# One level against two levels of Strassen's method in the second matmul of a linear-attention and feed-forward kernel

## The chip, the core and the metric

The kernel runs on one core of a Trainium2 chip. The metric is the device time of one launch in microseconds (us). All arithmetic is in 32-bit floats. TensorE (PE) multiplies; its weight loads have a row of their own in the profile (PEld). VectorE (DVE), ScalarE (ACT) and GpSimd (POOL) do the elementwise work. SyncE (SP) and ACT issue the DMAs.

## The reference, cut to what matters

```python
q, k, v: (8, 8, 576, 64)  float32     # batch, heads, sequence, head_dim
w_in: (512, 2048), w_out: (2048, 512) # float64: float32 normals times a float64 scalar

kv  = einsum('bhsd,bhse->bhde', k, v)
out = einsum('bhsd,bhde->bhse', q, kv)
out = out / sqrt(mean(out**2, -1) + 1e-6) * g_norm
x   = out, tokens by (head, dim)      # (4608, 512)
h   = x @ w_in                        # (4608, 2048)
g   = maximum(0.01 * h, h)
return (g @ w_out).astype(float32)    # (4608, 512)
```

## The kernel before, in words

**Blocks.** The 4608 tokens are cut into nine blocks of 512. For each batch entry of 576 tokens the attention writes its normalised output, transposed, into the `xT` tiles of the blocks that it touches. The feed-forward part then takes block after block. d_ff is cut into four units `c` of 512 (two halves `h` of 256 each: `w1_sb[h][c]`, `w2_sb[h][c]`).

**The first block** (`first_block`) is multiplied in the plain way: 16 slices of 128 of d_ff, each with four `h_ps` matmuls (L86) of 512 columns, a leaky ReLU on ACT (`gT`, L560) and four `o_acc` matmuls. While it runs, the weights arrive as 64-bit floats (`load_w`, 32 jobs of 0.5 MB, SP queue, L168) and `round_w` makes 32-bit floats of them: two ACT operations (L191, L193) and four DVE operations (L194, L197, L198, L200) for each job. `between(n, half)` hands out these jobs and the attention steps of batch entry 1 among the slices.

**The other eight blocks** use one level of Strassen's method (Winograd's form: seven products in place of eight) in both matmuls. `product_h` makes the seven products of a unit for h, `product_o` the seven for the output; each product is four matmuls of 256 columns. The profile shows every one of these matmuls as two MATMUL records and two LDWEIGHTS records. So a product, a "step", is eight records, a unit is 14 steps, and there are 32 units.

- The sums of weight quarters (`sides_w1`, `sides_w2`, tiles `ws`, `wt`) are made on POOL anew in every unit: eight operations of 128x512. The sums of the activations (`sides_g`, tiles `gs`) are four more. All elementwise sums go through the helper `add` (L400).
- The PSUM results go into `g11`..`g22` (ACT copies, DVE adds, ReLU on ACT) and into the output accumulators `o` (ACT copies when fresh, else DVE adds of 128x512).
- Finished accumulators go to DRAM from the ACT queue (L538).

**Order.** The main loop writes the order out: one h step, the rest of the o steps of the unit before, five h steps, one o step, the last h step, five o steps; the attention steps of the next batch entry (`a_steps`) stand between them. Matmuls (L86), `load_pair` DMAs and the rounding are pinned to program order; other instructions are ordered by the scheduler at build time, on each engine once and for all. The engines then run strictly in that order.

**Buffers.** POOL's weight sums live in `wcomb` tiles `pair0` to `pair3`, which during the first block also hold raw 64-bit weights; temporaries of the rounding live in the `gs` tiles. There are eight PSUM banks: `ha hb hc oa ob oc` and two for attention.

Of the kernel before, what the change touches and what calls it, by code (L numbers as in the profile page):

```python
# [8 lines left out]
F32 = mybir.dt.float32  # L9
# [13 lines left out]
def kernel(  # L23
# [28 lines left out]

    nc = tc.nc
# [19 lines left out]
    stage = ctx.enter_context(tc.tile_pool(name="stage", bufs=3))  # L73
# [3 lines left out]
    wcomb = ctx.enter_context(tc.tile_pool(name="wcomb", bufs=1))  # L77
    gpool = ctx.enter_context(tc.tile_pool(name="gpool", bufs=2))
    opool = ctx.enter_context(tc.tile_pool(name="opool", bufs=2))
# [5 lines left out]
    def matmul(*args, **kw):  # L85
        pin(nc.tensor.matmul(*args, **kw))  # L86

# [30 lines left out]
    def load_first():  # L118
# [4 lines left out]
        def rows(t):  # L123
# [5 lines left out]
        ks, vs = (t + [rows(wcomb.tile([P, 4 * U * P], F32, tag=f"pair{i + j}",  # L129
                                       name="early_kv")) for i in range(2)]  # L130
                  for j, t in ((0, ks), (2, vs)))
        for way, to, src, ts, p in (
# [8 lines left out]
    zeros = gpool.tile([P, NT], F32, tag="g11", name="zeros")  # L141
# [7 lines left out]
    w2_sb = [[consts.tile([P, U, DM], F32, name=f"w2_{h}_{c}") for c in range(NC)]  # L149
             for h in range(2)]  # L150

    spare_homes = itertools.cycle(("gs1", "gs2", "gs3", "gs4"))

    def spare(n, name, dtype=F32):

        return gpool.tile([P, n], dtype, tag=next(spare_homes), name=name)

    raw_homes = itertools.cycle([(stage, "raw")] * 3 + [(wcomb, f"pair{i}") for i in range(4)])
# [11 lines left out]
    def load_f64(src):  # L170
        a, n = src.shape[-2:]
        n //= 2
        pool, tag = next(raw_homes)
        raw = pool.tile([P, a * n, 2], U32, tag=tag, name="raw")
        load(raw.rearrange("p (a n) two -> p a (n two)", a=a), src)
        return raw

    def round_f64(dst, raw):
# [11 lines left out]
        add = spare(a * n, "add", U32)  # L190
# [130 lines left out]
    def attention(b):  # L321

        qT = qTs[b] = work.tile([P, NP, S], F32, tag="qT", name="qT")
        kv_ps = kv_tiles()
        for p in range(NP):
            q_in = q_ins.pop((b, p))
            nc.vector.transpose(  # L327
                qT[:, p, :].rearrange("p (t s) -> p s t", s=T),
                q_in.rearrange("p (s d) -> p s d", d=D)[:, :, :32])
            if p % 2 == 0:  # L330
                yield
                continue
            attention_kv(b, p // 2, kv_ps)
            for i in (p - 1, p):
                nxt = (b, i + 2) if i + 2 < NP else (b + 1, i + 2 - NP)
                if nxt[0] < B:
                    load_pair(*nxt)
            yield
        copy_kv(b, kv_ps)
        yield  # L340
        for i in (b, b + 1):
            yield from tail_of(b, max(i * NT, b * S), min((i + 1) * NT, (b + 1) * S))

    def first_attention():


        idle = ps_m.tile([P, NT], F32, tag="ob", name="idle_ps")
# [8 lines left out]
        rest = [ps_m.tile([P, NP // 2, 64], F32, tag=t, name="rest_ps") for t in ("oc", "oa")]  # L356
        for j in range(3):
            load_w(j)
        for p in range(NP):
            q_in = q_ins.pop((0, p))  # L360
            q_ps = ps_m.tile([P, J - 1, 64], F32, tag=("ha", "hb", "hc", "ha")[p], name="q_ps")
# [21 lines left out]
        free = iter(("ha", "hb", "hc", "oa", "ob", "oc", "ha", "hb"))  # L383
# [5 lines left out]
        for e in range(2):  # L389
            outputs(0, 0, N2, e, sums[0], ps, spare)  # L390
        outputs(0, N2, NT, 0, sums[1], ps, spare)
        divide(0, N2, sums[0], spare)
        outputs(0, N2, NT, 1, sums[1], ps, spare)
        divide(N2, NT, sums[1], spare)
# [7 lines left out]
    def sides_w1(c):  # L402

        a11, a12 = w1_sb[0][c][:, :, :2, :], w1_sb[0][c][:, :, 2:, :]
        a21, a22 = w1_sb[1][c][:, :, :2, :], w1_sb[1][c][:, :, 2:, :]
        s12, s34 = (wcomb.tile([P, 2, U, 2, P], F32, tag=f"pair{i}", name=f"ws{i}")
                    for i in range(2))
        s1, s2, s3, s4 = s12[:, 0], s12[:, 1], s34[:, 0], s34[:, 1]
        add(nc.gpsimd, s1, a21, a22)
        add(nc.gpsimd, s2, s1, a11, True)  # L410
        add(nc.gpsimd, s3, a11, a21, True)
        add(nc.gpsimd, s4, a12, s2, True)
        return {1: a11, 2: a12, 3: s4, 4: a22, 5: s1, 6: s2, 7: s3}

    def sides_w2(c):
# [3 lines left out]
        t12, t34 = (wcomb.tile([P, 2, U, N2], F32, tag=f"pair{i}", name=f"wt{i}")  # L419
                    for i in range(2, 4))  # L420
        t1, t2, t3, t4 = t12[:, 0], t12[:, 1], t34[:, 0], t34[:, 1]
# [4 lines left out]
        return {1: b11, 2: b21, 3: b22, 4: t4, 5: t1, 6: t2, 7: t3}  # L426

    def sides_x(x):

# [8 lines left out]
        add(nc.vector, t4, b21, t2, True)  # L438
        return {1: b11, 2: b21, 3: b22, 4: t4, 5: t1, 6: t2, 7: t3}

    def sides_g(g):

        g11, g12, g21, g22 = g
        s1, s2, s3, s4 = (gpool.tile([P, U, N2], F32, tag=f"gs{i}", name=f"gs{i}")
                          for i in range(1, 5))
        add(nc.gpsimd, s1, g21, g22)
        add(nc.gpsimd, s2, s1, g11, True)
        add(nc.gpsimd, s3, g11, g21, True)
        add(nc.gpsimd, s4, g12, s2, True)
        return {1: g11, 2: g12, 3: s4, 4: g22, 5: s1, 6: s2, 7: s3}  # L450

    BANK = {1: "a", 6: "a", 7: "a", 4: "a", 2: "b", 5: "c", 3: "c"}

    def strassen(which, left, right, done):


        banks = {}
        for i in (1, 5, 2, 6, 3, 7, 4):
            first = BANK[i] not in banks
            if first:  # L460
                banks[BANK[i]] = ps_m.tile([P, 2, N2], F32, tag=f"{which}{BANK[i]}",
                                           name=f"{which}_{BANK[i]}")
            bank = banks[BANK[i]]
            for part in range(2):
                for r in range(2):
                    matmul(bank[:, part, :], lhsT=left(i, part, r), rhs=right(i, part, r),
                           start=first and part == 0 and r == 0, stop=(r == 1),
                           skip_group_check=True)
            done(i, bank)
            yield  # L470

    def product_h(c, x_sides, to):

        w_sides = sides_w1(c)
        g11, g12, g21, g22 = (gpool.tile([P, U, N2], F32, tag=f"g{i}", name=f"g{i}")
                              for i in ("11", "12", "21", "22"))
# [4 lines left out]
        def done(i, bank):  # L481
# [3 lines left out]
            elif i == 5:  # L485
                nc.scalar.copy(g22, bank)
# [3 lines left out]
            elif i == 6:  # L490
                nc.scalar.copy(g21, bank)
            elif i == 3:
                add(nc.vector, g21, bank, g21)
                relu(g21)
            elif i == 7:
                add(nc.vector, g22, bank, g22)
                relu(g22)
            else:
                relu(g12, bank)
                to.append(sides_g((g11, g12, g21, g22)))  # L500

        yield from strassen("h", lambda i, part, r: w_sides[i][:, part, r, :],
                            lambda i, part, r: x_sides[i][:, r, :], done)

    def product_o(c, g_sides, os, finish):
        w_sides = sides_w2(c)
        if c == 0:
            for key in ("11", "12", "21", "22"):
                os[key] = opool.tile([P, 2, N2], F32, tag="o", name=f"o{key}", bufs=6)

        def acc(key, bank, fresh):
            if c == 0 and fresh:
                nc.scalar.copy(os[key], bank)
            else:
                add(nc.vector, os[key], bank, os[key])

        def done(i, bank):
            for key, fresh in {1: [("11", True)], 5: [("22", True)], 2: [("11", False)],
                               6: [("12", True)], 3: [("12", False)], 7: [("22", False)],
                               4: [("21", True)]}[i]:  # L520
                acc(key, bank, fresh)
                if c == NC - 1 and {"11": 2, "12": 3, "22": 7, "21": 4}[key] == i:
                    finish(key, os[key])

        yield from strassen("o", lambda i, part, r: g_sides[i][:, r, part * P:(part + 1) * P],
                            lambda i, part, r: w_sides[i][:, r, :], done)
# [7 lines left out]
    def store(i):  # L534
        def finish(key, o):
            r0 = i * NT + (int(key[0]) - 1) * N2
            c0 = (int(key[1]) - 1) * N2
            nc.scalar.dma_start(  # L538
                out[r0:r0 + N2, c0:c0 + N2].rearrange("(t p) m -> p t m", p=P), o)
        return finish  # L540

    def first_block(between):

        accs = [ps_m.tile([P, DM], F32, tag=t, name="o_acc") for t in ("ha", "hb", "oa", "ob")]
        x, last = xTs.pop(0), None
        for n in range(2 * NC * U + 1):
            now = last
            if n < 2 * NC * U:
                c, h, u = n // (2 * U), n // U % 2, n % U
                h_ps = ps_m.tile([P, NT], F32, tag=("hc", "oc")[n % 2], name="h_ps")  # L550
# [103 lines left out]
```

## Time and profile before

| | |
|---|---|
| median of 3 runs (987.89 to 992.26) | 992.06 us |
| the profiled execution's own time | 991.89 us |
| its span | 990.2 us |
| PE, PEld busy | 958.0, 763.8 us |
| DVE, ACT, POOL busy | 435.3, 268.1, 499.0 us |
| DMA read, written | 53.1, 9.4 MB |
| first block's matmuls | 26.6 to 151.2 us |

The profile is one execution. Its time lies 1.7 us above its span and 0.2 us below the median. PE's busy time is the sum of records that overlap: a record's end is modelled and reaches into the next one. The distance from one start to the next is the price of a record: 0.216 us for 256 columns.

### The profile page before, as it was taken

How to read it: one execution, taken by the hardware profiler on the slowest of the kernel's cores; microseconds unless marked ns; L12 is line 12 of the kernel's file. 1: busy time of each engine (PE TensorE's matmuls, PEld its weight loads, DVE VectorE, ACT ScalarE, POOL GpSimd, SP SyncE). 2: the span in 40 equal slices, each digit the busy share in tenths (PEclk: the TensorE clock that was granted, in tenths of full speed). 3: DMA queues.
4: the chain of work that ended last, by engine and by line, in shares of the span. 5: the costliest groups of instructions: out<-in, count | busy, mean ns of one | idle time of the engine just before them, and what ended most of it. 6: DMA issues, size and time to landing. Idle time of an engine off the chain costs nothing.

```text
span 990.2 us, 14098 instructions
## 1 busy us (share of the span) xinstructions
PE 958.0 (97%) x5702; PEld 763.8 (77%) x5702; DVE 435.3 (44%) x688; ACT 268.1 (27%) x531; POOL 499.0 (50%) x395
## 2 busy tenths in 40 slices
PE   8899987999999999999999999999999999999997
PEld 4444435878887888888887888788878888888885
DVE  3968971264234533364335433552245322422223
ACT  3645432331124211421133113311242112112210
POOL 1000214455655665566556666565556666666642
PEclk9899999999999999999999999999999999999999
DMA  9989505300260008000610043003100010001001
GB/s 251 243 214 239 164 1 138 96 1 1 56 178 1 1 2 231 2 1 1 178 56 1 1 121 113 1 1 96 45 1 1 1 43 1 1 1 43 1 1 42
DMA packets 36160, 63.47 MB, mean 64 GB/s; under 512 B 4864, under 2 KB 21248, under 8 KB 36096
## 3 DMA queue, kind: packets, MB, share of 16 engines
q1 hardware_dynamic: 26112, 51.95, 19.9%
q10 hardware_dynamic: 9856, 10.62, 3.2%
q8 instruction: 45, 0.74, 0.3%
q14 instruction: 19, 0.16, 0.1%
q0 software_dynamic: 128, 0.00, 0.0%
HBM read 53.12 MB, written 9.44 MB: 63 GB/s over the span
## 4 chain that ended last, share of the span: by engine, by line
PE 90%; DVE 6%; DMA 2%; ACT 1%; issue 1%; SPq 0%; ACTq 0%; DVEq 0%
PE h_a L86 22%; PE o_a L86 21%; PE h_c L86 11%; PE o_c L86 11%; PE h_b L86 6%; PE o_b L86 6%; PE o_acc L86 5%; PE h_ps L86 5%; PE kv_ps L86 2%; PE o_ps L86 2%; DVE qT L327 1%; DVE sum L289 1%; DMA k_in<-in_k_dram 1%; DMA v_in<-in_v_dram 1%; DMA raw<-in_moe_w_in_dram 1%
## 5 line engine op out<-in xcount | busy, mean ns | idle before, releaser
L400 DVE TENSOR_TENSOR o<-o_a,o 128x512 f32<-128x512 f32 x104 | 71.5, 688 | 122.2 <-PE o_a L86 122.2
L86 PE MATMUL o_a<-wt,gs 128*128 128x256 f32 x512 | 122.1, 381 | 0.0
L400 POOL TENSOR_TENSOR ws<-w 128x512 f32<-128x512 f32 x32 | 44.3, 1385 | 136.6 <-PE h_a L86 97.1
L400 POOL TENSOR_TENSOR wt<-w,w 128x512 f32<-128x512 f32 x32 | 40.9, 1277 | 140.5 <-PE o_a L86 137.4
L86 PEld LDWEIGHTS o_a<-wt,gs 128*128 128x128 f32 x512 | 96.3, 190 | 15.2 <-issue 2.1
L479 ACT ACTIVATE g<-g 128x512 f32<-128x512 f32 x96 | 60.5, 630 | 167.4 <-DVE g L400 167.4
L400 POOL TENSOR_TENSOR gs<-g,g 128x512 f32<-128x512 f32 x64 | 81.3, 1270 | 23.0 <-ACT g L479 22.5
L400 POOL TENSOR_TENSOR ws<-w,w 128x512 f32<-128x512 f32 x32 | 41.9, 1310 | 97.4 <-DMA raw<-in_moe_w_in_dram 94.6
L484 ACT COPY g<-h_a 128x512 f32<-128x512 f32 x32 | 18.7, 585 | 255.5 <-PE h_a L86 244.4
L400 POOL TENSOR_TENSOR wt<-w,wt 128x512 f32<-128x512 f32 x64 | 83.4, 1303 | 2.5
L400 POOL TENSOR_TENSOR wt<-w 128x512 f32<-128x512 f32 x32 | 41.2, 1289 | 65.6 <-PE o_a L86 60.0
L86 PE MATMUL h_a<-xt,w 128*128 128x256 f32 x256 | 62.6, 388 | 7.8 <-DVE g L400 7.8
L86 PE MATMUL h_ps<-xT,w 128*128 128x512 f32 (+1 forms) x136 | 60.5, 589 | 8.1 <-DVE xT L308 4.8
L400 DVE TENSOR_TENSOR g<-h_b,g 128x512 f32<-128x512 f32 x32 | 22.1, 689 | 98.0 <-PE h_b L86 98.0
L400 DVE TENSOR_TENSOR o<-o_c,o 128x512 f32<-128x512 f32 x56 | 38.4, 685 | 57.6 <-PE o_c L86 57.6
L86 PE MATMUL o_a<-wt,g 128*128 128x256 f32 x256 | 60.8, 380 | 1.9 <-DVE o L400 1.9
L86 PE MATMUL h_a<-xT,ws 128*128 128x256 f32 x256 | 62.4, 386 | 0.0
L86 PEld LDWEIGHTS h_a<-xt,w 128*128 128x128 f32 x256 | 48.8, 193 | 17.2 <-DVE g L400 10.6
L86 PE MATMUL h_a<-xT,w 128*128 128x256 f32 x256 | 62.0, 386 | 0.0
L86 PE MATMUL o_a<-w,g 128*128 128x256 f32 x256 | 60.6, 379 | 0.8 <-DVE o L400 0.8
L86 PE MATMUL h_a<-xt,ws 128*128 128x256 f32 x256 | 61.1, 382 | 0.0
L86 PE MATMUL o_c<-wt,gs 128*128 128x256 f32 x256 | 60.8, 381 | 0.0
(86 smaller groups left out, 1741.1 us busy)
## 6 DMA issues: line engine op xcount, KB each, us to landing
out_dram<-o ACTq DMA_DIRECT2D x36, 256.0 KB, 2.2
v_in<-in_v_dram SPq DMA_DIRECT2D x30, 288.0 KB, 5.0
raw<-in_moe_w_in_dram SPq DMA_DIRECT2D x64, 128.0 KB, 5.5
raw<-in_moe_w_out_dram SPq DMA_DIRECT2D x16, 512.0 KB, 6.2
k_in<-in_k_dram SPq DMA_DIRECT2D x28, 288.0 KB, 3.5
q_in<-in_q_dram SPq DMA_DIRECT2D x56, 144.0 KB, 4.5
q_in<-in_q_dram SPq DMA_DIRECT2D x56, 140.0 KB, 4.6
k_in<-in_k_dram ACTq DMA_DIRECT2D x2, 288.0 KB, 9.2
```

Of the source, the lines that this page charges most:

```text
L86: pin(nc.tensor.matmul(*args, **kw))
L289: nc.vector.tensor_add(sums[l], sums[l], sq)
L327: nc.vector.transpose(qT[:, p, :].rearrange("p (t s) -> p s t", s=T), q_in.rearrange("p (s d) -> p s d", d=D)[:, :, :32])
L400: eng.tensor_tensor(out_, a, b_, op=ALU.subtract if minus else ALU.add)
L479: nc.scalar.activation(t, t if src is None else src, func=AF.Prelu, alpha=SLOPE)
L484: nc.scalar.copy(g11, bank)
```

## The change

The first matmul keeps one level of Strassen's method. The second gets two: every product of halves becomes seven products of quarters, 49 in a unit, each one matmul of 128x128 by 128 columns. For every j of the outer seven (a "step" again) these are four matmuls into a PSUM tile `o_a` (128x512) and three into `o_b` (128x384).

- **Weights.** All sums of weights are made once: `sum_w1` (four POOL sums) and `sum_w2` (four POOL sums, three ACT copies, eight DVE sums) for each of the four units, handed out by `between` as soon as all rounding jobs have been handed out. The blocks are written to DRAM tiles (`w1_dram`, `w2_dram`: 4 and 14 DMAs for a unit, 1.05 and 3.21 MB, SP queue) and are read back for every block of tokens into rings: `w1_ring` with 6 places, `w2_ring` with 5, each read issued when the step that used the place is done.
- **Activations.** `sides_g` makes the second level's sums: eight POOL operations (four of 512, four of 384 columns) on top of the four of the first level.
- **Accumulators.** Each o step adds `o_a` and `o_b` into `acca` and `accb` (DVE, or ACT when fresh). `outputs_of` combines the seven second-level products after the last unit: 28 DVE sums of 128x128 for a block, then the store, now from the SP queue (the last block: SP and ACT).
- **Order.** h and o steps alternate, one of each; an attention step follows every second pair.
- **Places.** The pools `stage`, `wcomb`, `gpool`, `opool` are gone; fixed places serve several uses. The `tall` tile of `sum_w2` is a single place in `w2_ring`, overlapping two of the eight places for raw weights; the `w2_sb` tiles share places with `ga` and `acca`.

```diff
-    def sides_w1(c):   ...
-    def sides_w2(c):   ...
+    def sum_w1(c):
+        a11, a12, a21, a22 = w1_blocks(c)
+        s = {i: view(spare(NT, "ws"), 0, U, 2, P) for i in (1, 2, 3, 4)}
+        add(nc.gpsimd, s[1], a21, a22)
...
+    def sum_w2(c):
+        b11, b12 = w2_sb[0][c][:, :, :N2], w2_sb[0][c][:, :, N2:]
+        b21, b22 = w2_sb[1][c][:, :, :N2], w2_sb[1][c][:, :, N2:]
+        tall = {"a": view(w2_ring, 7 * P, 4, U, N2), "b": view(w2_ring, 7 * P + 4 * U * N2, 3, U, N2)}
+        t1, t2, t3, t4 = tall["a"][:, 3], tall["b"][:, 0], tall["b"][:, 2], tall["a"][:, 2]
+        add(nc.gpsimd, t1, b12, b11, True)
+        add(nc.gpsimd, t2, b22, t1, True)
+        add(nc.gpsimd, t3, b22, b12, True)
+        add(nc.gpsimd, t4, b21, t2, True)
+        nc.scalar.copy(tall["a"][:, 0], b11)
+        nc.scalar.copy(tall["a"][:, 1], b21)
+        nc.scalar.copy(tall["b"][:, 1], b22)
+        for g, n in (("a", 4), ("b", 3)):
...
+            add(nc.vector, u1, c12, c11, True)
+            add(nc.vector, u2, c22, u1, True)
+            add(nc.vector, u4, c21, u2, True)
+            add(nc.vector, c12, c22, c12, True)
+        def write():
+            for j in ORDER:
+                for g, lo, hi in (("a", 0, 4), ("b", 4, 7)):
+                    pin(nc.sync.dma_start(w2_dram[c][j][:, lo:hi, :], terms[g][j]))
...
+    def product_o(q, g_sides):
+        for t, j in enumerate(ORDER):
+            w = o_place(7 * q + t)
+            for g, lo, tags in (("a", 0, ("o0", "o1")), ("b", 4, ("o2", "o3"))):
...
+                for m in range(n):
+                    matmul(bank[:, m, :], lhsT=g_sides[g][j][:, m, :], rhs=w[:, lo + m, :],
+                           start=j in FRESH and m == 0, stop=True, skip_group_check=True)
+                to = accs[g][:, kl]
+                if c == 0 and fresh:
+                    nc.scalar.copy(to, bank)
+                else:
+                    add(nc.vector, to, bank, to)
+            read_o(7 * q + t + R2)
+            if c == NC - 1 and j in (2, 7, 3, 4):
+                outputs_of(i, kl, accs)
+            yield
+    def outputs_of(i, kl, accs):
...
+        for to, a in ((p2, p1), (p6, p1), (p7, p6), (p6, p5), (p4, p7), (p7, p5), (p3, p6)):
+            add(nc.vector, to, to, a)
...
     def between(n, half):
...
+        if rounded == len(w_jobs):
+            todo = next(sums, None)
+            if len(writes) > 1 or todo is None and writes:
+                writes.pop(0)()
+            if todo:
+                writes.append(todo[0](todo[1]))
...
     first_block(between)
+    for n in range(R1):
+        read_h(n)
+    for write in writes:
+        write()
+    for n in range(R2):
+        read_o(n)
...
+            for t in range(7):
+                go(h_steps, 1)
+                go(o_steps, 1)
+                if (7 * c + t) % 2:
+                    go(a_steps, 1)
```

## The prediction

> **What bounds the kernel now.** I read the busy times, the chain of waits, stretches of the span, prices of single groups, and last the timeline around the stage that changes.
>
> ```profile
> PE 958.0 (97%) x5702; PEld 763.8 (77%) x5702; DVE 435.3 (44%) x688; ACT 268.1 (27%) x531; POOL 499.0 (50%) x395
> PE 90%; DVE 6%; DMA 2%; ACT 1%; issue 1%; SPq 0%; ACTq 0%; DVEq 0%
> 100.00:125.00 25.00, 25.00 (x101) 10.18 (x100) 23.37 (x35) 11.58 (x24) 5.54 (x4) 1.00 0.54 147
> 125.00:151.00 26.00, 23.39 (x69) 9.82 (x68) 19.29 (x33) 7.40 (x17) 4.42 (x3) 1.00 0.03 10
> 151.00:230.00 79.00, 69.98 (x481) 57.33 (x480) 29.12 (x46) 23.36 (x48) 37.97 (x30) 0.94 0.27 71
> 430.00:534.00 104.00, 102.87 (x655) 87.05 (x654) 44.27 (x68) 26.55 (x54) 61.42 (x48) 1.00 0.21 56
> ```
>
> TensorE is 97% busy and 90% of the chain. The last four lines are stretches (length; busy us of PE, weight loads, DVE, ACT, POOL; granted clock; DMA share; GB/s). In the eight Strassen blocks PE has no air, while DVE, POOL and DMA have much. In the first block DVE is nearly full up to 125 us. Prices next: groups (count, sum in us, mean ns, idle before), one kind of DMA (us to landing), and rows of the timeline (start us, us, engine):
>
> ```profile
> L400 DVE TENSOR_TENSOR o<-o_a,o 128x512 f32<-128x512 f32 x104 | 71.5, 688 | 122.2 <-PE o_a L86 122.2
> L400 POOL TENSOR_TENSOR gs<-g,g 128x512 f32<-128x512 f32 x64 | 81.3, 1270 | 23.0 <-ACT g L479 22.5
> L400 DVE TENSOR_TENSOR xt<-xT 128x512 f32<-128x512 f32 x8 | 10.2, 1277 | 7.2 <-PE h_c L86 7.2
> L400 DVE TENSOR_TENSOR xT<-xT 128x512 f32<-128x512 f32 x8 | 5.5, 690 | 0.2
> L289 DVE TENSOR_TENSOR sum<-sum,sq 128x128 f32<-128x128 f32 x4 | 1.0, 273 | 0.0
> out_dram<-o ACTq DMA_DIRECT2D x36, 256.0 KB, 2.2
> 92.58 1.80 SPq L168 DMA_DIRECT2D raw<-in_moe_w_in_dram  x4
> 142.82 0.60 ACT L560 ACTIVATE gT<-h_ps 128x512 f32<-128x512 f32 x1 [3.91 <-PE h_ps L86]
> 141.97 1.59 POOL L400 TENSOR_TENSOR ws<-w,ws 128x512 f32<-128x512 f32 x1
> 142.47 1.64 DVE L200 CUSTOM_DVE_ANT_0 w<-w,add 128x1024 uint16<-128x1024 uint16 x1
> 145.66 0.69 DVE L200 CUSTOM_DVE_ANT_0 w<-w,add 128x1024 uint16<-128x1024 uint16 x1
> 264.69 1.28 PE L86 MATMUL kv_ps<-v_in,k_in 64*64 64x64 f32 x72
> 701.68 1.89 PE L86 MATMUL h_c<-xt,ws 128*128 128x256 f32 x8
> 703.41 0.81 PE L86 MATMUL h_b<-xT,w 128*128 128x256 f32 x3
> 706.65 1.70 PEld L86 LDWEIGHTS h_c<-xT,ws 128*128 128x128 f32 x8
> 708.95 1.59 PEld L86 LDWEIGHTS h_a<-xT,ws 128*128 128x128 f32 x8
> ```
>
> A DVE operation with two SBUF operands takes 0.69 us alone and 1.2 to 1.6 us while POOL works (the two L200 rows, one beside a POOL sum; the two `xT` groups); one that reads PSUM stays at 0.69. An SP issue costs 0.45 us. A step of eight records lasts 703.41 - 701.68 = 1.73 us, 0.216 us each. The two weight-load rows differ by 0.11 us: after a pause the second load starts 0.108 us after the first, so a 128-column load occupies 0.108 us and is hidden under 0.216 us of streaming.
>
> **The change part by part.**
>
> *The o step.* 28 matmuls of 256 columns become 49 of 128 for a unit: 14 records in a step in place of eight, half as long. Streaming is 0.216 / 2 = 0.108 us, and so is the load: the cover that hid loads is gone, both must run at once without a seam. The nearest row is `kv_ps`: 64-column loads before 64-column matmuls on four quarters of the array, 18 records on each in about 1.06 us (1.28 less the 0.22 us of a record's tail), 0.059 us each where streaming alone is 0.216 x 64/256 = 0.054. So a record costs 0.108 at best, 0.118 by that ratio; I take 0.110, as the excess looks like a fixed few ns. A step: 14 x 0.110 = 1.54 us against 1.73; 224 steps save 42 us (17 to 48). PE is on the path, so this counts in full.
>
> [...]
>
> *POOL.* A unit loses eight weight sums (8 x 1.27) and gains four `sides_g` sums of 512 and four of 384 (about 9 us): 14 us of work in a 24 us unit. The new place on the path: step 0 of o needs the first-level sum s4. From product 3's end: 0.27 to DVE, 0.69 add, 0.63 ReLU, four sums at 1.25, so 3.4 us after product 4; the `o_b` matmuls that read it start 1.54 + 1.73 + 0.88 = 4.2 us after it. 0.7 us to spare. The h products now share two PSUM banks in place of three; an o step of 1.54 us stands between uses, which hides the 0.6 us ACT copy that frees the bank. Without that cover it would cost some 0.5 us a step.
>
> *DVE.* The adds of a unit grow from 4.8 to 7 x (0.69 + 0.55) = 8.7 us, h keeps 2.1, `outputs_of` brings 28 x 0.27 = 7.6 us a block (18 beside POOL). With 17 us for attention a block asks 68 to 78 of 98 us. It fits, but in order: the 28 sums and the transposes stand before adds that free PSUM. I put 1.5 us of PE waiting on a block, 12 in all (0 to 40).
>
> *DMA.* 4.26 MB of weight blocks a unit: with q, k, v and the store 21.6 MB a block, 220 GB/s over 98 us. The busiest long stretch before moved 251 GB/s. Rings reach five steps ahead, 16 us. Hidden, with an eighth of air. On SP the reads now queue behind `load_pair`, which waits for PE's kv matmuls, and behind the store, which waits for the last `outputs_of` (some 5 us on DVE): both shorter than 16 us, so nothing is charged.
>
> *The stage between first block and second.* Here is the loss. On SP all 72 weight writes stand before the first read, and each `sum_w2` waits for the one before: `tall` is a single place, and POOL's first sum of the next unit waits for the writes out of it. The first `sum_w2` waits in turn for raw weights in the same place, whose last rounding stands on ACT behind the last `gT`. Walking that order:
> - last `gT` ends 143.4 (row); two roundings on ACT at 0.67: 144.8; three POOL sums at 1.4: 149.0;
> - DVE: the last rounding operation, eight sums (half beside POOL: 4 x 1.25 + 4 x 0.6 = 7.4), two `o_acc` copies: 158; two issues and 2.2 us landing: 161;
> - two rounds of POOL 3.8 + DVE 7.4 + issues 0.9 + landing 3 = 15.1: 191; the last one without landing, 11.2, and five issues: 204.7;
> - the first read queues behind some 1.8 MB of writes, about 5 us: 209.7.
>
> PE waits some 6 us for that last rounding, does two products of unit 0 (they need no new sums) and then stands; the 6 us vanish in the stall. Product 6, third of its unit, starts at 209.7, where the third product before started at 154.6: 55 us later. Bounds: all sums alone and 2.2 us landings give 196; all beside POOL and landings of 6 us give 230.
>
> *The end.* The last o unit has no h beside it: DVE needs 8.7 + 7.6 us for it, PE 10.8. The end comes 10.5 us after PE's last record, before 4.5.
>
> *The sum*, against the span of 990.2: 209.7, then 222 h steps x 1.727 = 383.4, 224 o steps x 1.54 = 345, attention matmuls 31 (as now), gaps that stay 19 (of 24.9 now; the waits for k and v near 170 us fall into the stall), new waits 12, PE's slower clock after standing 2 (the 151 to 230 stretch shows 0.94 around a 5 us wait), the end 10.5: 1012.6. With the 1.7 us around the span 1014, against 991.9 for that execution and a median of 992.1.
>
> **The rivals.**
>
> *A, not slower: the write chain overlaps.* If POOL alone set the pace (eight sums at 1.28 = 10.2 us a round, everything else beside it), product 6 would start at 149 + 3 x 10.2 + 12 (the last DVE sums, issues, landing) = 192, and the time is 997. From there down every us counts: with records at 0.108 and no new waits it is 978. For it: DMA is at 3% and POOL nearly idle from 125 to 151. Against: `tall` has one place, and the waits stand in the built order. It decides from a third product at 192 or earlier.
>
> *B: DVE or the reads bound the blocks.* If `outputs_of` and attention queue before the adds, or reads that share the engines with q, k and v fall under 200 GB/s (21.6 MB then need 108 us a block), each block costs 3 to 9 us more: 1035 to 1080. For it: the order on DVE is fixed, and GB/s fell to 147 at a share of 0.54 in the stretch from 100 us, the same 270 at full share. Against: that same 270.
>
> *C: the load is not hidden.* Load and matmul in turn, 0.216 us a record: a step 3.02 us, 1.48 more than forecast, 224 times: 1345. For it: no row shows 128 columns on 128; against: the kv row.
>
> **How the numbers follow.** The forecast, 998 to 1034, has 0.62; A, 978 to 998, 0.20; B 0.13; C 0.05. About 0.5%, 5 us, is what a measurement of this kernel can tell from no change: 987 to 997 is "same". Half of A falls there and half below: faster 0.10, same 0.10, slower 0.80. The range leaves out C, the upper half of B and the bottom of A: 986 to 1046.
>
> **What would show it.** `o_a` records 0.110 us apart; PE standing from about 160 to 210 us with the chain through `tall`, its POOL and DVE sums and DMA writes; the granted clock dipping there; blocks of about 99 to 101 us after it; DVE the last engine at the end. Wrong, if the third product starts before 190, if o steps last over 1.65 us, or if blocks last over 104 us.

## The result, and the profile after

The changed kernel takes 1073.02 us (median of 4 runs, 1071.01 to 1074.70) against 992.16 us (4 runs, 987.89 to 995.70) beside it: the ratio is 1.0816, with a 95% interval of 1.0769 to 1.0863. The profiled execution took 1074.70 us, its span is 1073.0. Slower was right; the size was not: 1014 was forecast with a range up to 1046, so 59 us are missing, and the forecast span of 1012.6 falls 60.4 short.

The page of the kernel after, and then two of the stretches that were shown of before (length; busy us of PE, weight loads, DVE, ACT, POOL; granted clock; DMA share; GB/s):

```profile
PE 946.5 (88%) x7046; PEld 797.6 (74%) x7046; DVE 687.6 (64%) x1136; ACT 291.2 (27%) x575; POOL 500.1 (47%) x427
PE 62%; DVE 13%; DMA 12%; POOL 5%; issue 5%; ACT 2%; SPq 2%; ACTq 0%; DVEq 0%; POOLq 0%
```

```profile
151.00:230.00 79.00, 18.67 (x125) 13.22 (x126) 35.49 (x37) 8.54 (x16) 32.62 (x24) 0.61 0.80 269
430.00:534.00 104.00, 98.30 (x748) 89.13 (x747) 74.12 (x118) 29.06 (x58) 56.76 (x48) 0.98 0.73 214
```

TensorE falls from 97% of the span to 88%, and from 90% of the chain to 62%. The first stretch is the stage that was foreseen: 18.67 us of matmuls in 79 us. The second is one of the eight blocks, and it is the surprise: 98.30 busy us in 104, at a clock of 0.98, where the same stretch before had 102.87 at 1.00. What TensorE waits for, in total, times and the longest:

```profile
PE h_ps L87 <- DMA w_ring<-w1s: 56.1, 1, 56.1
PE o_a L87 <- DVE acca L435: 33.5, 7, 4.8
PE o_b L87 <- POOL gb L435: 8.9, 8, 2.0
```

The first is the stage. The second comes once in each of seven blocks with the same length: from the last `h_ps` record to the next `o_a` record it is 4.95 us more than their spacing, seven times. The timeline around one of them (start us, us, engine), from one product before the wait to the slow matmuls behind it:

```profile
434.38 0.28 DVE L435 TENSOR_TENSOR accb<-accb,acca 128x128 f32<-128x128 f32 x1
436.01 1.27 POOL L435 TENSOR_TENSOR ga<-g,ga 128x512 f32<-128x512 f32 x1 [10.36 <-ACT g L545]
436.25 1.17 DVE L435 TENSOR_TENSOR acca<-acca 128x128 f32<-128x128 f32 x1
437.23 1.32 POOL L435 TENSOR_TENSOR gb<-ga,g 128x512 f32<-128x512 f32 x1
437.27 1.05 PE L87 MATMUL o_a<-w_ring,ga 128*128 128x128 f32 x8
437.35 1.35 DVE L435 TENSOR_TENSOR accb<-accb,acca 128x128 f32<-128x128 f32 x1
438.83 1.89 PE L87 MATMUL h_ps<-xT,w 128*128 128x256 f32 x8
...
443.51 1.35 DVE L435 TENSOR_TENSOR accb<-accb,acca 128x128 f32<-128x128 f32 x1
444.78 0.68 DVE L435 TENSOR_TENSOR acca<-o_a,acca 128x512 f32<-128x512 f32 x1
445.51 1.57 PE L87 MATMUL o_a<-w_ring,ga 128*128 128x128 f32 x8 [4.79 <-DVE acca L435]
...
448.15 2.57 PE L87 MATMUL h_ps<-xT,w 128*128 128x256 f32 x8
```

Up to 434.4 us the sums of `outputs_of` follow each other every 0.20 to 0.33 us. At 436.01 POOL begins the sums `s1` to `s4` and `sides_g`, and from there each DVE sum of 128x128 begins 0.1 to 0.25 us after one of POOL's and ends some 0.15 us after that one does, 1.07 to 1.35 us in all. Seven of them take 8.5 us; at 0.20 us each they would take 1.4. The transfers do not explain it: the DMA share is 1.00 while the quick sums run (432.9 to 434.6 us) and 1.04 beside the slow ones. Behind them on DVE stands the add that frees the bank `o_a`, which itself, reading PSUM, takes its usual 0.68. And after the wait TensorE is slow: eight `o_a` records in 1.57 us instead of 1.05, eight `h_ps` records in 2.57 instead of 1.89.

The stage, in the chain of waits (start us, us), from the second round on:

```profile
168.12 1.28 POOL w_ring L435
...
185.14 1.27 POOL w_ring L435
...
202.40 1.27 POOL w_ring L435
...
216.72 3.64 DMA w_ring<-w1s
220.49 1.62 PE h_ps L87 x3
```

POOL's first sum into the single place `tall` starts at 168.12, 185.14 and 202.40: rounds of 17.0 and 17.3 us, each through POOL, DVE, the issues and a landing. Product 6 starts at 220.5.

### The profile page after: what moved, and what is told of

Its sections match the earlier page's. It is cut to its first block, busy times and chain, and to the rows that moved or that the text cites. A ratio compares the mean times of both kernels' runs of the same rounds, so it can differ in the third digit from the quotient of the medians.

```text
span 1073.0 us, 18534 instructions
## 1 busy us (share of the span) xinstructions
PE 946.5 (88%) x7046; PEld 797.6 (74%) x7046; DVE 687.6 (64%) x1136; ACT 291.2 (27%) x575; POOL 500.1 (47%) x427
## 4 chain that ended last, share of the span: by engine, by line
PE 62%; DVE 13%; DMA 12%; POOL 5%; issue 5%; ACT 2%; SPq 2%; ACTq 0%; DVEq 0%; POOLq 0%
PE h_ps L87 31%; PE o_a L87 16%; PE o_b L87 12%; DVE accb L435 5%; DMA q_in<-in_q_dram 4%; DVE acca L435 2%; DMA gb<-in_moe_w_in_dram 2%; POOL gb L435 2%; PE o_ps L87 2%; DMA w_ring<-in_moe_w_in_dram 2%; DMA w_ring<-w2s 2%; POOL w_ring L435 2%; PE kv_ps L87 1%; SPq L493 1%; DMA k_in<-in_k_dram 1%
## 5 line engine op out<-in xcount | busy, mean ns | idle before, releaser
L435 DVE TENSOR_TENSOR acca<-o_a,acca 128x512 f32<-128x512 f32 x192 | 131.4, 684 | 130.4 <-PE o_a L87 126.2
L87 PE MATMUL h_ps<-xT,w 128*128 128x256 f32 (+1 forms) x648 | 193.0, 445 | 5.3 <-DVE xT L339 4.3
L87 PE MATMUL h_ps<-xt,w_ring 128*128 128x256 f32 x512 | 124.1, 386 | 56.1 <-DMA w_ring<-w1s 56.1
L87 PEld LDWEIGHTS h_ps<-xT,w 128*128 128x128 f32 x648 | 126.8, 205 | 55.1 <-issue 30.9
L87 PEld LDWEIGHTS o_a<-w_ring,sa 128*128 128x128 f32 x1024 | 134.1, 192 | 9.4 <-issue 1.7
L87 PE MATMUL o_a<-w_ring,ga 128*128 128x128 f32 x768 | 108.9, 288 | 33.7 <-DVE acca L435 33.5
L87 PE MATMUL o_a<-w_ring,sa 128*128 128x128 f32 x1024 | 135.1, 275 | 2.6 <-issue 1.5
L87 PEld LDWEIGHTS o_a<-w_ring,ga 128*128 128x128 f32 x768 | 106.3, 202 | 41.8 <-DVE acca L435 37.1
L87 PE MATMUL h_ps<-xT,w_ring 128*128 128x256 f32 x512 | 121.5, 381 | 0.0
L87 PE MATMUL o_b<-w_ring,sb 128*128 128x128 f32 x768 | 106.7, 275 | 0.0
L87 PEld LDWEIGHTS o_b<-w_ring,gb 128*128 128x128 f32 x576 | 77.4, 203 | 10.8 <-POOL gb L435 10.7
```

The costliest lines, as they stand in the source:

```text
L435: eng.tensor_tensor(out_, a, b_, op=ALU.subtract if minus else ALU.add)
```

## The experiments

All were timed in three rounds beside the kernel before, whose median was 993 to 994 us in each group. The theory after reading the trace: the foreseen chain through `tall`, and in the blocks a queue on DVE (theory P): seven small sums beside POOL's, at 1.07 to 1.35 us each instead of 0.20, make `o_a` wait 4.95 us for `acca` at the start of seven blocks. Each wait then costs TensorE some clock too: around its end the granted clock falls to 0.50 for 3.4 or 6.8 us (the half clock), put at 2.25 us a wait; the trace gives 16 us behind the seven, 2.3 each.

**The sums left out.**

```diff
-        for to, a in ((p2, p1), (p6, p1), (p7, p6), (p6, p5), (p4, p7), (p7, p5), (p3, p6)):
-            add(nc.vector, to, to, a)
```

> Left out: the 28 sums of `outputs_of` per block (the store still sends the accumulators). [...] Without them 7 x (4.95 + 2.25) = 50 us go in the blocks and 3 to 4 us at the end: 1073 becomes 1018 to 1022, and the blocks last 96 to 99 us. Rival D (DMA reads or the q/k/v landings hold the blocks, the DVE wait only shows it): the wait stays or moves to a DMA, 1060 or more.

Measured: 1017.25 us (1015.72 to 1018.89), ratio 1.0235 (1.0213 to 1.0257). The wait for `acca` is gone from all blocks, and no DMA wait takes its place. One stretch of this run:

```profile
430.00:530.00 100.00, 100.00 (x837) 91.34 (x836) 56.39 (x94) 29.69 (x59) 57.58 (x50) 1.00 0.78 234
```

So 55.8 us hang on 28 sums a block that take 5.6 us on DVE when nothing disturbs them (28 x 0.20), and the transfers, at 234 GB/s in this stretch, do not bound the blocks. The blocks with attention beside them lasted 98 to 104 us, where 96 to 99 was expected; the waits of `o_b` for `gb`, 8.1 us, are still there.

**The sums a unit later, order left to the scheduler.**

```diff
-            if c == NC - 1 and j in (2, 7, 3, 4):
+            if i == NB - 1 and c == NC - 1 and j in (2, 7, 3, 4):
                 outputs_of(i, kl, accs)
             yield
+        if i < NB - 1 and c == NC - 1:
+            late.extend((i, kl, accs) for kl in (0, 3, 1, 2))
...
+                for _ in range((0, 0, 1, 2, 1, 0, 0)[t]):
+                    if late:
+                        outputs_of(*late.pop(0))
```

> Nothing left out. The sums of `outputs_of` and the store come one unit later, in steps 2 to 4 of the next unit, where POOL stands in the trace (some 451.5 to 467 us of the third block). Theory P: each of the 28 sums takes 0.20 to 0.28 us there, the wait and the half clock go as in the run without sums, only the end stays: 1021 to 1025. Rival Q (28 more DVE operations are simply too much DVE work for a block): the wait moves with the sums and stays about as large, 1060 to 1075.

Measured: 1068.99 us (1068.69 to 1069.59), with the wait where it was: 32.1 us in seven. The time lies in Q's band, but the wait did not move with the sums as Q says. In the trace DVE runs the sums in almost the same places as before the edit: they depend only on finished accumulators, and the scheduler put them back a unit. The edit did not do what it said, so it tells nothing on P or Q.

**The same, pinned.** The sums are tied behind the instruction that precedes them in the program.

```diff
-            add(nc.vector, to, to, a)
+            pin(nc.vector.tensor_tensor(to, to, a, op=ALU.add))
```

> Nothing left out. As the run with late sums, but the 28 sums are pinned behind the instruction before them, so that the scheduler cannot put them back: on DVE they now stand behind the adds of step 1 of the next unit, where POOL has done its sums. Theory P: 0.20 us each, the 4.95 us wait and the half clock behind it go in all seven blocks (7 x 7.2 = 50 us), the end stays: 1073 becomes 1020 to 1027. Rival Q (too much DVE work in a block, wherever it stands): the waits come back at other steps, 1050 or more.

Measured: 1021.56 us (1020.17 to 1022.31), ratio 1.0294 (1.0272 to 1.0316). Of the 21 sums in the first lump 18 last 0.28 to 0.31 us and three, beside POOL's last sums, about 1.1. Two neighbours from the timeline of this run, with POOL's last sum:

```profile
443.46 1.05 POOL L435 TENSOR_TENSOR sb<-gb,sb 128x384 f32<-128x384 f32 x1
443.68 0.98 DVE L641 TENSOR_TENSOR accb<-accb,acca 128x128 f32<-128x128 f32 x1
444.58 0.28 DVE L641 TENSOR_TENSOR acca<-acca,accb 128x128 f32<-128x128 f32 x1
```

The three that still meet POOL cost nothing, as the DVE adds behind them are not due: in these two steps ACT copies the fresh accumulators. The same work, in another place, takes 51 us less. It is not the amount of DVE work.

**Half the width.**

```diff
-            add(nc.vector, to, to, a)
+            add(nc.vector, to[:, :64], to[:, :64], a[:, :64])
```

> Left out: half of each sum of `outputs_of` (64 of 128 columns). Theory P (a DVE operation on two SBUF operands beside POOL lasts until a POOL operation ends, whatever its size): the seven sums beside POOL stay at 1.24 to 1.35 us, the wait at 4.8 to 4.95, the time within 4 us of 1073. Rival S (price by size, stretched by sharing): they halve to 0.6 to 0.7 us, the wait shrinks to 0.5 us, the half clock with it, 1025 to 1035.

Measured: 1065.13 us (1063.42 to 1067.22). The rows beside POOL, with half the elements:

```profile
437.83 1.26 POOL L435 TENSOR_TENSOR gb<-ga 128x512 f32<-128x512 f32 x1
437.99 1.19 DVE L435 TENSOR_TENSOR accb<-accb 128x64 f32<-128x64 f32 x1
439.21 1.31 DVE L435 TENSOR_TENSOR accb<-accb,acca 128x64 f32<-128x64 f32 x1
```

Six of the seven last as long as with 128 columns, 1.03 to 1.31 us here and 1.07 to 1.35 there. The rival, price by size, falls: beside POOL a sum of 64 columns costs about one POOL operation (1.03 to 1.32 us in the timeline above), as one of 128 does. What holds the sums back does not show, and other widths were not tried. The wait shrank to 4.25 us, not to 0.5; the first of the seven lasted 0.75 us instead of 1.17. The time came out 4 us under the expected band. Seven waits shorter by 0.70 us are 4.9 of the 7.9 us to the kernel after, and the end behind PE's last record is 1.3 us shorter; the rest was not followed up.

**The wait filled with other matmuls.**

```diff
                 go(h_steps, 1)
+                if i > 1 and c == 1 and t == 0:
+                    idle = ps_m.tile([P, NT], F32, tag="h1", name="idle_ps")
+                    w = w1_sb[0][0]
+                    for _ in range(5):
+                        matmul(idle, lhsT=w[:, 0, 0, :], rhs=w[:, 0].rearrange("p e m -> p (e m)"),
+                               start=True, stop=True)
                 go(o_steps, 1)
```

> Nothing left out; seven times five matmuls of 512 columns (4.3 us) on old weights are added in front of the `o_a` step that waits 4.95 us for `acca`, into a PSUM bank that is free there. The wait of DVE itself is not changed. Theory K (a TensorE that stands some 5 us is granted half the clock for some 3 us after it, which is 1.9 to 2.9 us of each 7.2 us loss): with TensorE busy the granted clock stays at 1.00 there and 7 x 2.25 = 16 us go: 1055 to 1059. Rival L (the slow records behind the wait come from the late DVE, not from the clock, or the clock falls with the load whatever is run): 1070 to 1076.

Measured: 1056.52 us (1056.04 to 1058.18), 16.5 us less for doing more. TensorE's rows behind the wait, to be held against those of the kernel after above:

```profile
444.99 1.16 PE L87 MATMUL o_a<-w_ring,ga 128*128 128x128 f32 x8 [0.53 <-DVE acca L435]
...
446.66 1.89 PE L87 MATMUL h_ps<-xT,w 128*128 128x256 f32 x8
```

And the granted clock over 4.5 us behind the wait, first in the kernel after, then with the wait filled:

```profile
445.50:450.00 4.50, 4.49 (x20) 4.17 (x21) 4.43 (x6) 1.06 (x2) 4.50 (x5) 0.62 0.35 105
```

```profile
444.90:449.40 4.50, 4.41 (x32) 4.20 (x33) 4.43 (x7) 1.06 (x2) 4.50 (x5) 1.00 0.50 162
```

A wait of 4.95 us thus costs 7.3 on average: 2.36 us (16.5 / 7) are the clock that is taken away afterwards, where 2.25 was put down. The trace of the kernel after agrees and shows how uneven it is: over the 10 us behind each of the seven waits the granted clock is 0.69 to 0.86, which is 1.4 to 3.1 us of clock at one wait and 16 in all. With the wait filled it is 1.00 from 444.9 to 454.4 us, and the mean over the span is 0.961 instead of 0.942. Half clock behind two waits of `o_b` for `gb`, 10.2 us in the kernel after, can hold a part of the difference too. The 16.5 us is a difference between runs of different groups, and the times in each spread by 2 to 4 us.

**Two places for `tall`.**

```diff
-        tall = {"a": view(w2_ring, 7 * P, 4, U, N2), "b": view(w2_ring, 7 * P + 4 * U * N2, 3, U, N2)}
+        if c % 2:
+            tall = {"a": view(w2_ring, 7 * P, 4, U, N2), "b": view(w2_ring, 7 * P + 4 * U * N2, 3, U, N2)}
+        else:
+            tall = {"a": view(w1_ring, 0, 4, U, N2), "b": view(gb_place, 0, 3, U, N2)}
```

> Nothing left out. `tall` gets a second place (units 0 and 2 in `w1_ring` and `gb`, units 1 and 3 where it was). Theory T (the single place makes a chain of POOL, DVE, issues and landing, 17.0 us a round): rounds overlap, and what stays is POOL's eight sums (10 to 12 us) or 4.26 MB at the 330 GB/s of the busiest stretch (12.9 us). Three rounds of 13 in place of 17 and a first round that can start 2 to 3 us earlier: product 6 starts at 203 to 209 in place of 220.5 us, time 1057 to 1062. Rival V (the 17 MB of writes at about 250 GB/s set the pace, whatever the order of the sums): rounds stay at 16 to 17 us, 1068 to 1075.

Measured: 1066.24 us (1061.68 to 1070.13; the profiled execution is the fastest). Product 6 starts at 210.3 us, 10.2 earlier, a little later than expected. Two of the four times lie near 1062 and two near 1070, so the gain in time is 3 to 11 us against the median of the kernel after, and its size is open. A stretch of the stage in the kernel after, then the first and the last of four in this run:

```profile
170.00:180.00 10.00, 0.00 (x0) 0.00 (x0) 8.02 (x5) 0.00 (x0) 9.49 (x7) 0.50 0.60 199
```

```profile
170.00:180.00 10.00, 0.00 (x0) 0.00 (x0) 8.19 (x10) 1.45 (x3) 3.25 (x3) 0.51 1.01 325
...
200.00:210.00 10.00, 0.00 (x0) 0.00 (x0) 0.00 (x0) 0.00 (x0) 0.00 (x0) 0.50 0.99 311
```

Both theories hold a part. The single place set the pace in the kernel after, where the DMA share was 0.60 to 0.91 between 170 and 210 us. Without it the next bound is right behind: the writes, 17 MB, at a full share and 311 to 340 GB/s from 170 to 210 us, with DVE and POOL done by 200.

**A plain second block.**

```diff
-    first_block(between)
+    first_block(0, between)
+    first_block(1, between_1)
+    go(a2)
...
-    for i in range(1, NB):
+    for i in range(2, NB):
```

`between_1` hands out the attention steps of batch entry 2 and then, from slice 3 on, one sum of weights and one set of writes in a slice.

> Nothing left out. The second block is multiplied in the plain way too (16 slices, 110.6 us of streaming), and the sums of weights with their writes go on beside it; seven blocks stay with Strassen's method. Theory T: the stall of 56 us is only the chain of sums and writes, and it hides under the plain block; the third block then starts at about 150 + 110.6 + 4 = 265 us in place of 327, and one of the seven 7 us waits goes too: 1073 - 62 - 6.5 = 1004 (1000 to 1015). Rival W (the cost of the preparation is resources, not order: writes and sums slow the matmuls of the block beside them): 1025 to 1050.

Measured: 1026.61 us (1025.15 to 1028.21), ratio 1.0334 (1.0313 to 1.0355). There is no wait for `w1s` left, and the plain block has no air in it, at a DMA share of 0.71:

```profile
160.00:276.00 116.00, 115.53 (x470) 51.92 (x469) 42.62 (x60) 23.00 (x49) 32.91 (x23) 1.00 0.71 228
```

The third block's first product starts at 276.1 us, where 265 was expected: the plain block begins 9 us later than assumed, since the wait for the last rounding, 5.5 us, stays in front of it; half clock behind that wait, as in the kernel after (0.50 from 152.5 to 159.4 us, 3.4 us of clock), would be the rest. The 327 that the expectation set against it for the kernel after was too late. There the third block's first product starts at 309.7, and the seven o steps left of the second, some 11 us, still stand among its products, which puts it at some 321. The start thus gained 45 us, not 62, and the time came out at 1026.6, not 1004. That lies within W's band, but W's mechanism does not show: the matmuls of the plain block run without a pause beside the sums and the writes. The cost of the preparation is its place in the order.

**`sides_x` two steps later.**

```diff
-                if c == NC - 1 and t == 4 and i + 1 < NB:
+                if c == NC - 1 and t == 6 and i + 1 < NB:
```

> Nothing left out. The last attention steps and the sums `sides_x` for the next block come at step 6 of the last unit in place of step 4. Theory G (the waits of `o_b` for `gb`, 8.9 us, and the half clock behind them come from the DVE add of product 3, which stands behind `sides_x` and so starts POOL's sums late): most of them go, 5 blocks x 2.5 to 3 us: 1056 to 1064. Rival H (the attention's own DVE operations, not `sides_x`, make that add late, or the wait only moves to product 6 of the next block, which needs `sides_x`): 1068 to 1078.

Measured: 1067.86 us (1065.58 to 1069.96). The waits of `o_b` for `gb` fall from 8.9 to 4.0 us, and those for `acca` rise from 33.5 (7 times) to 36.3 (9 times). The time lies between the theories, 0.1 us under H's band; the difference to the kernel after is 5 us, and the intervals of the two ratios (1.0733 to 1.0790, 1.0769 to 1.0863) overlap: inconclusive as to size.

**Three edits together**: the plain second block, the pinned late sums, the late `sides_x`.

> Nothing left out. The plain second block, the pinned late sums and the late `sides_x` together. If the three losses are separate and add: 1026.6 - 6 x 7.2 - 13 = 970 (962 to 985), under the kernel before. If they cover one another, or if a TensorE that stands less is granted less clock later: 985 to 1005.

Measured: 977.64 us (975.60 to 981.54), ratio 0.9864 (0.9829 to 0.9900): 15.5 us under the kernel before. It lies in the band expected for losses that add (962 to 985): 1026.61 less six times 7.3 (43.8) is 982.8, and the 5 us of the late `sides_x`, whose size is unsettled, would make it 977.8.

```profile
PE 942.0 (97%) x6694; PEld 742.9 (76%) x6694; DVE 573.5 (59%) x1046; ACT 280.4 (29%) x557; POOL 442.6 (45%) x379
```

TensorE is at 97% again, as before the change.

## Why the prediction was right or wrong

- **The record of the o step: right.** Eight `o_a` and six `o_b` records start 0.111 us apart (433.98 to 437.27 us is one pair of steps, 3.29 us; 1.727 + 1.54 were forecast). The two hundredths, over some 220 pairs, make 5 us.
- **The stage: right mechanism, 10.8 us too short.** Product 6 came at 220.5, forecast 209.7, within the bound of 230. POOL began at 147.1 instead of 144.8; the first round ended at 168.1 instead of 161: behind DVE's last sum stood five issues of SP, 4.2 us, where two, 0.9, were put down, and two of them took 1.2 us each at a DMA share of 0.98; the landing took 4.3 instead of 2.2. The later rounds took 17.0 to 17.3 instead of 15.1. In the sum the 17 MB of writes appeared only as landings; at the 325 GB/s of the run with two places they alone would take some 52 us.
- **DVE in the blocks: the step that failed.** "I put 1.5 us of PE waiting on a block, 12 in all (0 to 40)." The amount of work was right (74.1 us in 104; 68 to 78 were forecast), and the danger was named: sums before adds that free PSUM. But a sum beside POOL was priced at 18 / 28 = 0.64 us, as if it shrank with its width. The rows of before showed the stretching at 512 columns only, 1.2 to 1.6 us, and nothing in them said that 128 columns last 1.07 to 1.35 us as well. Seven sums in a row make 8.5 us, not 4.5 (7 x 0.64), and the queue in front of TensorE is 4.95 us in seven blocks: 34.7 us. By these numbers 4 us less of sums would have left a wait of 0.9, inside the 1.5 that was put down. From one of these waits to the next it is 104.7 to 113.0 us for the blocks with attention beside them, and 100.1 for the last: over the 104 that the prediction named as a sign of being wrong.
- **The clock: failed too.** Two us were put down for the stage alone. The waits in the blocks bring 16.5 us more, as the filled wait shows. Together with the waits this is 51 us, against 14 forecast for waits and clock.
- **POOL's 0.7 us to spare: wrong in one unit of a block.** Product 3's add can stand behind `sides_x` and the attention on DVE; then `s4` is late and `o_b` waits up to 2.0 us, 8.9 in all. It was not priced.
- **Rival B** had the right size (1035 to 1080) and half of the right cause: the queue on DVE, yes; the reads, no. It was given 0.13. The range ended at 1046 and so left out three quarters of it, not the upper half, as the prediction says; and its 3 to 9 us a block over eight blocks would be 1038 to 1086.
- **The end**: 7.7 us after PE's last record starts; 10.5 were forecast.
- The account: 10.8 (stage), 5 (records), 37 (waits and clock over the 14 forecast), 8.9 (`gb`), 3 less at the end, together 59 of 60.4.

## What to carry to other kernels

Price small VectorE sums beside GpSimd by the number of instructions, not by elements (here 1.03 to 1.31 us each at 64 columns, 1.07 to 1.35 at 128), and ask where in the order they fall: the same 28 sums a block cost 51 us more in one place than a few steps later. A wait of TensorE of 4.95 us cost here half as much again in clock on average, so a queue is worth more than its length. Work that prepares a long phase belongs under matmuls that need nothing of it, even if these take the dearer way: the plain second block cost some 18 us more matmul time (110.6 against 92 for a block) and saved 46, one of the seven waits included.

## What the runs showed of the hardware that was not expected

The half clock after a short wait is not the same each time. In the kernel after, `o_b` waited 1.95 us for `gb` at 849 us, and the eight `h_ps` records behind it lasted 3.52 us, at a granted clock of 0.50 from 852.3 to 855.7 us; the same wait of 1.96 us at 236 us was followed by 1.89 us at 1.00:

```profile
238.57 0.71 PE L87 MATMUL o_b<-w_ring,gb 128*128 128x128 f32 x4 [1.96 <-POOL gb L435]
239.12 1.89 PE L87 MATMUL h_ps<-xT,w 128*128 128x256 f32 x8
...
851.63 0.71 PE L87 MATMUL o_b<-w_ring,gb 128*128 128x128 f32 x4 [1.95 <-POOL gb L435]
852.18 3.52 PE L87 MATMUL h_ps<-xT,w 128*128 128x256 f32 x8
```

In the run with pinned late sums the wait at 236 us, 1.96 us again, was followed by eight `h_ps` records in 3.46 us. Every stretch of half clock between 230 and 1000 us of the kernel after lasts 3.4 or 6.8 us.

No run shows why a wait of this length is followed by half clock at one time and by the full clock at another.
